# Agent attention and a SoLU feed-forward: the SBUF rings moved to multiples of 512 bytes

## The chip, the cores and the metric

The kernel runs on 1 core of a Trainium2 chip. The metric is the device time of one execution in microseconds (us), as the median of several runs; lower is better.

## What is computed

Agent attention over 4 sequences of 12608 tokens with 128 channels and 49 agents, and then a feed-forward layer with a softmax-gated activation (SoLU) and a layer norm over all 50432 rows:

```python
def sm(a, b):
    s = scale * (a @ b.transpose(0, 2, 1))
    e = np.exp(s - s.max(-1, keepdims=True))
    return e / (e.sum(-1, keepdims=True) + 1e-09)
agent_v = sm(agents, k) @ v
x = (sm(q, agents) @ agent_v).reshape(B * S, D)

h = x @ w_in                                   # 128 -> 1024
e = np.exp(h - np.max(h, axis=-1, keepdims=True))
solu = h * e / (np.sum(e, axis=-1, keepdims=True) + 1e-09)
mu = np.mean(solu, axis=-1, keepdims=True)
var = np.mean((solu - mu) ** 2, axis=-1, keepdims=True)
return ((solu - mu) / np.sqrt(var + 1e-06) * g_ln) @ w_out
```

## The kernel before

The rows are cut into 394 tiles of 128 tokens. For each sequence a first phase (`phase_a`) goes over k and v in chunks of 1024 tokens, held in the rings `kt` and `vt` (for the first sequence in the rings `x` and `t`, which are free then), and leaves agent_v, multiplied into w_in, as a pair of fp16 matrices `mh` and `ml`. A second phase (`phase_b`) makes the softmax of 8 tiles of q (ring `qt`) over the agents and turns it with PE into the fp16 tiles `pT`.

Then each tile runs through one chain. PE multiplies `pT` with `mh` and `ml` into the PSUM tile `ph` (line 953). DVE takes the row minimum and writes the scaled h to `e` (line 981). ACT takes the exponential (line 988). DVE multiplies to `u` (line 996). ACT squares for the variance into `sq` (line 1017). The last product needs u with its features on the partitions. For 343 of the 394 tiles this is done by DMA: POOL (now and then ACT) splits u into a high and a low fp16 half in a tile of the ring `f` (lines 1002 to 1007), and SP issues a DMA transpose from `f` to a tile of the ring `x` (line 1011), 512 KB of fp16 each. PE multiplies `x` with the weights `wh` and `wl` (line 1045). The other tiles are turned by PE into the ring `t` (lines 1024, 1029). DVE scales four tiles into `ob` (line 1092), and SP stores them (line 1096).

All DMAs are issued from SP's one queue, in order. The order of the work on every engine is a stored table (`STEPS`) that `Plan.run` reads; the planner's costs and due times don't set it.

What the change touches is where the tiles lie. Buffers that live throughout are taken one after another from the pool `const`, by `ring` for those that are used in turn. Within a partition each tile starts at the next multiple of 32 bytes behind the one before, so a tile of 4 bytes (one column) takes 32. The large tiles of the rings have 1024, 2048 or 4096 bytes per partition. In the kernel before the first ring, `e`, starts at byte 31200 of a partition, and the eight single columns `su` stand between `u` and `f`:

| tiles | bytes each | first byte before | above a multiple of 512 | of 256 | of 64 |
|---|---|---|---|---|---|
| win_sb, w32 | 4096 | 18816 | 384 | 128 | 0 |
| e, u | 4096 | 31200 | 480 | 224 | 32 |
| f, x, t, kt, vt, qt | 4096 | 64224 | 224 | 224 | 32 |
| ek, eT, ob | 2048 | 174816 | 224 | 224 | 32 |
| pT | 1024 | 183008 | 224 | 224 | 32 |
| mh, ml | 2048 | 202304 | 64 | 64 | 0 |
| sq | 2048 | 212672 | 192 | 192 | 0 |

`mh`, `ml` and `sq` come from other pools, which lie behind `const`. The tiles `ident`, `ones`, `ag_sb`, `wh16` and `wl16` lie ahead of the rings, like `win_sb`, at multiples of 64.

Of the kernel before, what the change touches and what calls it, by code (L numbers as in the profile page):

```python
# [13 lines left out]
F32 = mybir.dt.float32  # L14
# [221 lines left out]
def kernel(  # L236
# [14 lines left out]
    DF = w_in.shape[1]  # L251
    P = 128
    NF = DF // P
    HW = 512
    GT = 4
# [13 lines left out]
    UBUF = 6  # L269
# [4 lines left out]
    UB = 8  # L274
# [73 lines left out]
    const = ctx.enter_context(tc.tile_pool(name="const", bufs=1))  # L348
# [69 lines left out]
    def ring(m, shape, dt, name):  # L418
        return [const.tile(shape, dt, name=f"{name}_{chr(97 + i)}") for i in range(m)]

    er, ur, sur = ring(2, [P, DF], F32, "e"), ring(UBUF, [P, DF], F32, "u"), ring(8, [P, 1], F32, "su")
    fr_, xr, tr = ring(FBUF, [P, 2, DF], F16, "f"), ring(XB, [P, 2 * NF, P], F16, "x"), ring(TBUF, [P, NF, P], F32, "t")
    ktr, vtr, qtr = ring(2, [P, CT * P], F32, "kt"), ring(2, [P, CT * P], F32, "vt"), ring(2, [C, UB * P], F32, "qt")
    ekr, etr, ptr = ring(2, [P, HW], F32, "ek"), ring(2, [P, HW], F32, "eT"), ring(PTB, [P, GT * P], F16, "pT")
    obr, fcr = ring(2, [P, GT, P], F32, "ob"), ring(12, [P, 1], F32, "fc")
    mxr, smr = ring(4, [P, UB], F32, "mx"), ring(4, [P, UB], F32, "sm")
    words = {}
    wi, wo = w_in.bitcast(I32), w_out.bitcast(I32)

# [128 lines left out]
    def both(x):  # L558
        return seq[x][0] % 2 == 1 and seq[x][1] == 0

    mdone, mlast, last_h, ex, CB, cbs = {}, {}, {}, {}, {}, {}
    bmats = {}

# [728 lines left out]
```

## Time and profile before

| | |
|---|---|
| median of 3 runs | 1373.23 us (1370.92 to 1373.4) |
| the profiled execution | 1374.36 us |
| its span, first to last instruction | 1372.6 us |
| PE, DVE, ACT, POOL busy | 90%, 87%, 87%, 84% of the span |
| DMA | 287.70 MB, mean 210 GB/s |
| DMA packets under 512 bytes | 718400 of 753388 |
| granted TensorE clock, mean | 0.977 of full speed |

In the rows below, PE is TensorE's matmuls, PEld its weight loads, DVE VectorE, ACT ScalarE, POOL GpSimd and SP SyncE, which here only issues DMAs. The rows of a line or tile give the count, the shortest, median and longest duration in ns, and when the first and the last one started. The rows of stretches give, after each engine's busy us and count, the granted clock, the share of the 16 DMA engines' time that packets took (above 1 where packets of one engine overlap), and the GB/s moved. "DMA to landing" is the time from the start of the issue to the end of the transfer.

### The profile page before, as it was taken

How to read it: one execution, taken by the hardware profiler on the slowest of the kernel's cores; microseconds unless marked ns; L12 is line 12 of the kernel's file. 1: busy time of each engine (PE TensorE's matmuls, PEld its weight loads, DVE VectorE, ACT ScalarE, POOL GpSimd, SP SyncE). 2: the span in 40 equal slices, each digit the busy share in tenths (PEclk: the TensorE clock that was granted, in tenths of full speed). 3: DMA queues.
4: the chain of work that ended last, by engine and by line, in shares of the span. 5: the costliest groups of instructions: out<-in, count | busy, mean ns of one | idle time of the engine just before them, and what ended most of it. 6: DMA issues, size and time to landing. Idle time of an engine off the chain costs nothing.

```text
span 1372.6 us, 36571 instructions
## 1 busy us (share of the span) xinstructions
PE 1230.9 (90%) x14322; PEld 934.9 (68%) x14322; DVE 1198.8 (87%) x2187; ACT 1198.3 (87%) x2212; POOL 1154.1 (84%) x944
## 2 busy tenths in 40 slices
PE   8889989888988998988998988889989898888987
PEld 4566766666766676766776767666877676676766
DVE  6799979877988898987998897989989899989986
ACT  5699989887989898988989897989989899989997
POOL 3589978887897897887988887988889899989985
PEclk9999999999999999999999999999999999999999
DMA  9599999999999999999989999999999999999997
GB/s 366 183 216 211 240 225 201 235 171 204 194 186 226 223 221 233 216 210 223 185 162 221 216 243 208 213 235 225 212 208 194 192 200 188 206 189 170 194 186 155
DMA packets 753388, 287.70 MB, mean 210 GB/s; under 512 B 718400, under 2 KB 721984, under 8 KB 753216
## 3 DMA queue, kind: packets, MB, share of 16 engines
q1 hardware_dynamic: 753216, 285.38, 104.1%
q8 instruction: 112, 1.84, 0.5%
q14 instruction: 60, 0.49, 0.1%
HBM read 79.67 MB, written 25.82 MB: 77 GB/s over the span
## 4 chain that ended last, share of the span: by engine, by line
DMA 22%; ACT 18%; PE 17%; DVE 15%; POOL 15%; issue 12%; SPq 1%; POOLq 0%; DVEq 0%; ACTq 0%
ACT ph L988 8%; PE px L1045 7%; ACT sq L1017 7%; PE ph L953 5%; DVE e_b L981 4%; POOL f_a L1007 2%; DMA out_dram<-ob_a 2%; DVE e_a L981 2%; DMA x_g<-f_c 2%; POOL f_c L1007 2%; POOL f_d L1007 2%; POOL f_e L1007 2%; DMA x_c<-f_e 2%; PE px L652 2%; DVE u_c L996 1%
## 5 line engine op out<-in xcount | busy, mean ns | idle before, releaser
L981 DVE TENSOR_SCALAR_CACHE_REDUCE e_a<-ph,nk 128x1024 f32<-128x1024 f32 x197 | 251.8, 1278 | 43.7 <-PE ph L953 42.1
L981 DVE TENSOR_SCALAR_CACHE_REDUCE e_b<-ph,nk 128x1024 f32<-128x1024 f32 x197 | 251.8, 1278 | 34.5 <-PE ph L953 32.4
L988 ACT ACTIVATE ph<-e_a,nm 128x1024 f32<-128x1024 f32 x197 | 218.9, 1111 | 42.3 <-DVE e_a L981 41.5
L988 ACT ACTIVATE ph<-e_b,nm 128x1024 f32<-128x1024 f32 x197 | 219.0, 1112 | 38.8 <-DVE e_b L981 37.9
L1045 PE MATMUL px<-wh,x_c 128*128 128x128 f16 x688 | 76.1, 224 | 23.4 <-DMA x_c<-f_e 7.5
L1045 PEld LDWEIGHTS <-x_c 128*128 128x128 f16 x1032 | 64.7, 100 | 39.8 <-DMA x_c<-f_e 8.5
L1045 PE MATMUL px<-wh,x_g 128*128 128x128 f16 x688 | 75.3, 225 | 13.5 <-DMA x_g<-f_c 7.0
L996 DVE SCALAR_TENSOR_TENSOR u_a<-e_a,cb,ph 128x1024 f32<-128x1024 f32 x66 | 84.2, 1275 | 2.7 <-ACT ph L988 1.9
L996 DVE SCALAR_TENSOR_TENSOR u_c<-e_a,cb,ph 128x1024 f32<-128x1024 f32 x65 | 82.8, 1274 | 4.1 <-POOL f_e L1007 1.6
L996 DVE SCALAR_TENSOR_TENSOR u_d<-e_b,cb,ph 128x1024 f32<-128x1024 f32 x66 | 84.1, 1274 | 1.8 <-ACT ph L988 0.8
L996 DVE SCALAR_TENSOR_TENSOR u_f<-e_b,cb,ph 128x1024 f32<-128x1024 f32 x65 | 82.9, 1276 | 2.0 <-ACT ph L988 1.3
L996 DVE SCALAR_TENSOR_TENSOR u_b<-e_b,cb,ph 128x1024 f32<-128x1024 f32 x65 | 82.9, 1275 | 1.4 <-ACT ph L988 1.2
L996 DVE SCALAR_TENSOR_TENSOR u_e<-e_a,cb,ph 128x1024 f32<-128x1024 f32 x65 | 82.9, 1276 | 0.9 <-ACT ph L988 0.3
L1045 PE MATMUL px<-wh,x_e 128*128 128x128 f16 x688 | 74.2, 222 | 10.6 <-DMA x_e<-f_e 3.5
L1045 PEld LDWEIGHTS <-x_g 128*128 128x128 f16 x1032 | 65.3, 101 | 26.2 <-DMA x_g<-f_c 8.1
L1045 PE MATMUL px<-wh,x_f 128*128 128x128 f16 x688 | 72.7, 222 | 9.7 <-DMA x_f<-f_d 4.7
L1045 PEld LDWEIGHTS <-x_e 128*128 128x128 f16 x1032 | 63.4, 99 | 23.3 <-DMA x_e<-f_a 4.4
L1045 PE MATMUL px<-wh,x_a 128*128 128x128 f16 x688 | 73.6, 221 | 6.2 <-DMA x_a<-f_e 3.2
L1045 PE MATMUL px<-wh,x_h 128*128 128x128 f16 x672 | 72.4, 221 | 6.3 <-DMA x_h<-f_d 2.2
L1045 PEld LDWEIGHTS <-x_a 128*128 128x128 f16 x1032 | 63.4, 99 | 21.4 <-issue 6.0
L1045 PE MATMUL px<-wh,x_b 128*128 128x128 f16 x688 | 72.6, 221 | 5.8 <-DMA x_b<-f_b 2.6
L1045 PEld LDWEIGHTS <-x_b 128*128 128x128 f16 x1032 | 63.3, 98 | 20.9 <-issue 5.6
(459 smaller groups left out, 4736.4 us busy)
## 6 DMA issues: line engine op xcount, KB each, us to landing
out_dram<-ob_a SPq DMA_DIRECT2D x49, 256.0 KB, 3.3
out_dram<-ob_b SPq DMA_DIRECT2D x49, 256.0 KB, 3.3
qt_a<-in_qT_dram SPq DMA_DIRECT2D x24, 512.0 KB, 4.8
qt_b<-in_qT_dram SPq DMA_DIRECT2D x24, 512.0 KB, 4.6
kt_b<-in_kT_dram SPq DMA_DIRECT2D x18, 512.0 KB, 4.8
kt_a<-in_kT_dram SPq DMA_DIRECT2D x18, 512.0 KB, 4.6
vt_b<-in_v_dram SPq DMA_DIRECT2D x18, 512.0 KB, 4.7
vt_a<-in_v_dram SPq DMA_DIRECT2D x18, 512.0 KB, 4.9
```

The source lines that it names most:

```text
L652: nc.tensor.matmul(px[h * AP2 : (h + 1) * AP2, :C], eT[:w, o + h * AP2 : o + (h + 1) * AP2], vt[:w, t, :], start=all(z[0] != h for z in mm ...
L953: nc.tensor.matmul(ph[:, sl], w, m[:, sl], start=(q == 0), stop=(q == len(mm) - 1))
L981: nc.vector.tensor_scalar(out=nhs[x], in0=phs[x], scalar1=nks[k][:, j : j + 1], scalar2=None, op0=ALU.mult, op1=ALU.min, accum_out=nms[x])
L988: nc.scalar.activation(out=phs[x], in_=nhs[x], func=AF.Exp, scale=-1.0, bias=nms[x], accum_out=rs_[R]["S"][:, j : j + 1])
L996: nc.vector.scalar_tensor_tensor(out=u, in0=nhs[x], scalar=scal(x)[:, 4:5], in1=phs[x], op0=ALU.mult, op1=ALU.mult, accum_out=su)
L1007: nc.gpsimd.tensor_tensor(out=fs[x][:, 1, :], in0=us[x][0], in1=fs[x][:, 0, :], op=ALU.subtract)
L1017: nc.scalar.activation(out=sq, in_=u, func=AF.Square, bias=su, scale=-float(DF), accum_out=rs_[R]["Q"][:, j : j + 1])
L1045: nc.tensor.matmul(po, ut, wt[:, kf, :], start=(q == 0), stop=(q == len(mm) - 1))
```

## The change

A tile `pad` of 32 bytes per partition is taken from `const` ahead of the rings, and the rings of short tiles (`su`, `fc`, `mx`, `sm`) are taken after all others. Nothing reads or writes `pad`.

```diff
-    er, ur, sur = ring(2, [P, DF], F32, "e"), ring(UBUF, [P, DF], F32, "u"), ring(8, [P, 1], F32, "su")
+    pad = const.tile([P, 8], F32, name="pad")
+    er, ur = ring(2, [P, DF], F32, "e"), ring(UBUF, [P, DF], F32, "u")
     fr_, xr, tr = ring(FBUF, [P, 2, DF], F16, "f"), ring(XB, [P, 2 * NF, P], F16, "x"), ring(TBUF, [P, NF, P], F32, "t")
     ktr, vtr, qtr = ring(2, [P, CT * P], F32, "kt"), ring(2, [P, CT * P], F32, "vt"), ring(2, [C, UB * P], F32, "qt")
     ekr, etr, ptr = ring(2, [P, HW], F32, "ek"), ring(2, [P, HW], F32, "eT"), ring(PTB, [P, GT * P], F16, "pT")
-    obr, fcr = ring(2, [P, GT, P], F32, "ob"), ring(12, [P, 1], F32, "fc")
-    mxr, smr = ring(4, [P, UB], F32, "mx"), ring(4, [P, UB], F32, "sm")
+    obr = ring(2, [P, GT, P], F32, "ob")
...
+    sur, fcr = ring(8, [P, 1], F32, "su"), ring(12, [P, 1], F32, "fc")
+    mxr, smr = ring(4, [P, UB], F32, "mx"), ring(4, [P, UB], F32, "sm")
```

The rings `e`, `u`, `f`, `x`, `t`, `kt`, `vt`, `qt`, `ek`, `eT`, `pT` and `ob` now all start at multiples of 512 bytes: `e` at 31232, `f` at 64000, `ob` at 187904. Behind them `mh` starts at 202336 (96 above a multiple of 256, 32 above one of 64) and `sq` at 212704 (224 above a multiple of 256, 32 above one of 64). What lies ahead of the rings stays. Every engine's list of instructions, SP's DMAs among them, is the same in the same order.

## Rows read from the trace of the kernel before

**Rows 1.** The page: busy us, share of span, instructions of each engine

```profile
PE 1230.9 (90%) x14322; PEld 934.9 (68%) x14322; DVE 1198.8 (87%) x2187; ACT 1198.3 (87%) x2212; POOL 1154.1 (84%) x944
```

**Rows 2.** The page: the chain that ended last, by engine, by line

```profile
DMA 22%; ACT 18%; PE 17%; DVE 15%; POOL 15%; issue 12%; SPq 1%; POOLq 0%; DVEq 0%; ACTq 0%
ACT ph L988 8%; PE px L1045 7%; ACT sq L1017 7%; PE ph L953 5%; DVE e_b L981 4%; POOL f_a L1007 2%; DMA out_dram<-ob_a 2%; DVE e_a L981 2%; DMA x_g<-f_c 2%; POOL f_c L1007 2%; POOL f_d L1007 2%; POOL f_e L1007 2%; DMA x_c<-f_e 2%; PE px L652 2%; DVE u_c L996 1%
```

**Rows 3.** Busy time by stretch: the steady part

```profile
core 0: us, PE busy (x) PEld busy (x) DVE busy (x) ACT busy (x) POOL busy (x), PEclk, DMA share, GB/s
64.00:1300.00 1236.00, 1113.27 (x13110) 851.46 (x13109) 1097.96 (x1981) 1104.20 (x2027) 1072.47 (x855) 0.98 1.07 208
```

**Rows 4.** Line 1011, the transposes: their waiters, issue to landing

```profile
  PEld L1045: 97.4, 69
  PE px L1045: 78.0, 61
...
DMA to landing us min/median/max: 4.2/5.2/9.6
```

**Rows 5.** Tile ob_a: its first waiter, landing of its stores

```profile
  DVE ob_a L1092: 29.3, 13
...
DMA to landing us min/median/max: 1.5/3.2/7.1
```

**Rows 6.** Stretches of the head, 512 KB loads alone

```profile
8.00:12.00 4.00, 4.00 (x22) 2.36 (x21) 2.54 (x9) 2.43 (x5) 0.49 (x1) 1.00 1.02 413
12.00:16.00 4.00, 4.00 (x52) 2.44 (x50) 3.93 (x10) 1.98 (x4) 0.78 (x1) 1.00 1.03 416
24.00:28.00 4.00, 4.00 (x44) 2.50 (x42) 3.48 (x9) 3.52 (x9) 0.64 (x1) 1.00 1.03 410
```

**Rows 7.** Stretches with one late-started transpose alone

```profile
75.95:77.70 1.75, 1.75 (x20) 1.26 (x19) 1.75 (x5) 1.69 (x4) 1.75 (x1) 1.00 1.27 287
367.98:369.82 1.84, 1.22 (x19) 1.12 (x20) 1.75 (x3) 1.84 (x2) 1.61 (x2) 1.00 1.24 280
418.60:420.30 1.70, 1.18 (x19) 1.12 (x20) 1.70 (x5) 1.70 (x4) 1.50 (x5) 1.00 1.27 289
983.85:985.60 1.75, 1.75 (x23) 1.72 (x22) 1.70 (x4) 1.75 (x5) 1.03 (x2) 1.00 1.27 290
```

**Rows 8.** Stretches with one promptly started transpose alone

```profile
79.00:81.40 2.40, 2.33 (x21) 1.06 (x18) 2.40 (x6) 1.96 (x5) 2.40 (x2) 1.00 1.14 212
114.10:116.50 2.40, 2.40 (x35) 1.95 (x33) 2.35 (x5) 2.40 (x5) 2.32 (x3) 1.00 1.13 204
192.10:194.40 2.30, 2.30 (x21) 1.91 (x19) 2.04 (x4) 2.27 (x5) 0.00 (x0) 1.00 1.13 205
224.80:227.20 2.40, 2.40 (x31) 1.76 (x28) 2.40 (x6) 2.37 (x5) 2.40 (x3) 1.00 1.14 210
```

**Rows 9.** SP's DMA issues in time: start, SP time

```profile
77.77 1.88 SPq L1011 DMA_TRANSPOSE x_d<-f_d  x1
...
415.71 3.13 SPq L1011 DMA_TRANSPOSE x_a<-f_d  x1
```

**Rows 10.** Lines 476, 1120: DVE's two 128x1024 maxima, ns min/median/max

```profile
L476 DVE TENSOR_REDUCE wt<-f_e x1: 1209/1209/1209, 52.7 to 52.7; 128x1 f32<-128x1024 f32 x1
...
L1120 DVE TENSOR_REDUCE wm<-win_sb x1: 1211/1211/1211, 27.2 to 27.2; 128x1 f32<-128x1024 f32 x1
```

**Rows 11.** Line 399: POOL's writes of win_sb and f_e, ns

```profile
L399 POOL TENSOR_TENSOR win_sb<-u_b,e_a x2: 1273/1277/1281, 17.9 to 21.7; 128x512 f32<-128x512 f32 x2
...
L399 POOL TENSOR_TENSOR f_e<-u_f,e_a x2: 1268/1271/1274, 37.0 to 38.3; 128x512 f32<-128x512 f32 x2
```

**Rows 12.** ACT by line and form: busy us, mean ns

```profile
L625 ACT ACTIVATE ek_a<-px,nmp 128x512 f32<-128x512 f32 x24 | 16.2, 676 | 4.1 <-DVE nmp L611 2.8 <-PE px L599 1.4
...
L748 ACT ACTIVATE mh<-px,cb 128x512 f16<-128x512 f32 x8 | 5.4, 674 | 1.9 <-PE px L742 1.9
```

**Rows 13.** Lines 742, 599: fp32 matmuls of 512 columns, ns

```profile
L742 PE MATMUL px<-win_sb,av_dup x16: 592/593/677, 49.4 to 1048.4; 128*128 128x512 f32 x16
...
L599 PE MATMUL px<-kt_b,ag_sb x80: 222/593/644, 79.2 to 986.1; 128*64 128x512 f32 x72, 128*64 128x256 f32 x4, 128*64 128x64 f32 x4
```

**Rows 14.** Lines 632, 652: fp32 matmuls of 128 columns, ns

```profile
L632 PE MATMUL px<-ident,ek_a x100: 272/273/330, 11.4 to 984.5; 128*128 128x128 f32 x100
...
L652 PE MATMUL px<-vt_b,eT_b x300: 269/273/325, 104.5 to 1014.1; 128*64 128x128 f32 x148, 64*64 64x128 f32 x2
```

**Rows 15.** Line 953: fp16 matmuls that stream mh and ml, ns

```profile
L953 PE MATMUL ph<-mh,pT_b x160: 376/379/634, 66.1 to 1319.0; 128*128 128x512 f16 x160
L953 PE MATMUL ph<-ml,pT_b x160: 376/379/634, 66.3 to 1319.2; 128*128 128x512 f16 x160
```

## The prediction

> **What bounds the kernel now.** I read the page's busy shares first. PE, DVE, ACT and POOL stand at 90, 87, 87 and 84% of the span [rows 1], so no engine is free enough to give much and none is full. Next the chain that ended last: DMA has 22% of it, ACT 18, PE 17, DVE and POOL 15 each, issue 12 [rows 2]. The chain hops between engines and transfers; it never stays on one. Over the steady part, 64 to 1300 us, DVE is busy 1097.96 of 1236 us, which is 89%, PE 90%, and the DMA share is 1.07 at only 208 GB/s [rows 3]. A share over 1 means that packets of one DMA engine overlap, so the queue is hardly ever empty although few bytes move.
>
> Who waits for DMA? The transposes of line 1011: PE's weight loads wait 97.4 us and its matmuls 78.0 us in total for them, mostly the same time seen twice, and a transpose takes 4.2 us at least and 5.2 in the median from issue to landing [rows 4]. Behind them stand the output stores: DVE waits 29.3 us, 13 times, for a buffer ob_a to be stored [rows 5]. So faster DMA would have somewhere to go, and that is the only place where this change can win anything.
>
> **The change part by part.** The lists of instructions of all five engines are the same row for row; only addresses differ. What lay at 224 above a multiple of 256 (f, x, t, kt, vt, qt, ek, eT, pT, ob; e and u too, at 480 above a multiple of 512) lies at 0. What is allocated behind the large rings moves as well: mh and ml go from 64 to 96 above a multiple of 256, so from a multiple of 64 to 32 beside one; sq does the same. So there are three things to price: engines on realigned tiles, engines on the tiles that lose their multiple of 64, and DMA.
>
> *Engines on realigned tiles.* The trace holds pairs in which one side is already at a multiple of 64 (win_sb, ident, w32, mh) and the other is 32 beside one (f, ek, kt, vt). DVE takes its maximum over 128x1024 of f_e in 1209 ns and of win_sb in 1211 [rows 10]. POOL's product into f_e takes 1271 ns, into win_sb 1277 [rows 11]. ACT writes 512 values into ek_a in 676 ns (mean) and into mh in 674 [rows 12]. PE streams 512 fp32 columns of win_sb in 593 ns and of kt_b in 593 [rows 13], and 128 columns of ident or of vt_b in 273 [rows 14]. The odd side is nowhere slower by more than 2 ns. I take 0 for the realigned tiles; e and u, which no pair holds, are the same kind of operand.
>
> *Engines on mh, ml and sq.* For sq, an ACT write, the pair of rows 12 says 0. For mh and ml no row shows fp16 columns streamed from 32 beside a multiple of 64. The nearest rows are the fp32 pairs, which say 0. I take 0 and keep a price for the third rival below; a gain I exclude, since no pair shows the odd side faster by more than 6 ns in 1271.
>
> *Loads.* While 512 KB loads run alone into the odd addresses, they move 410 to 416 GB/s [rows 6], 1.27 us for one. There is no row of a load into an aligned ring. The best stretch against the middle one is worth under 1%, 0.01 us per load; I take 0, and as an upper end a tenth of a load, 0.13 us, an estimate. The 1.5 us of the quickest store [rows 5] is mostly not wire time: 256 KB at 413 GB/s would be 0.63 us.
>
> *Transposes.* Here the odd address could cost most, since a transpose reads f and writes x, both at 224 above a multiple of 256. Its 512 KB have two speeds with the very same layout. One that starts soon after its issue (x_d<-f_d, issued at 77.77 [rows 9], moving in the stretch from 79.0) runs at 204 to 212 GB/s [rows 8], some 2.5 us. One that had to stand behind another (x_a<-f_d, issued at 415.71 [rows 9], moving from 418.6) runs at 280 to 290 GB/s [rows 7], 1.81 us. So the usual speed isn't the limit of the addresses: something ahead of the data, by inference the supply of descriptors, holds a prompt transpose, and it has the same work after the change. Only late transposes run against the engines' own limit, and only there can alignment show. Lower end: 0. Upper end: the wire speed of the loads, 413 instead of 289 GB/s, which is 1.27 us instead of 1.81, 0.54 us saved per late transpose. I take 0, because the trace shows no sign that the address is what separates 289 from 413; short packets with a fixed cost each would look just the same.
>
> The Trainium skill has a rule that says otherwise: "DMA: Bandwidth & Descriptors", section "How a descriptor splits into AXI transactions", states that a transaction starts at a multiple of 256 bytes, and that a descriptor that starts elsewhere fetches from the boundary below and pays for the unused bytes. For a 256-byte piece at 224 that would be 480 bytes paid for 256, so 413 GB/s would become 220. The trace agrees in half: prompt transposes are below that, but the late ones, at 280 to 290, are well above what it allows.
>
> *The sum.* The profiled execution took 1374.36 us, its span 1372.6, the median of three runs is 1373.23. Engines 0, loads 0, transposes 0: the time stays, 1373 us against the median.
>
> **The rivals.**
>
> *Faster: late transposes speed up.* What speaks for it: DMA is 22% of the chain, 302 us, and less the stores' 2% (27 us) there are 275 us in transfers of about 5.2 us, some 50 links. If every link were late and saved 0.54 us, 27 us would leave the chain. What speaks against it: the floor of 4.2 us isn't touched; DVE is busy 89% of the steady part and PE 90%, so the next wait is close behind. If half of the links are late and half of what they save is passed on, 7 us are left: 1366 us, with 1346 as its extreme. By the rule of the Trainium skill's page "DMA: Bandwidth & Descriptors" quoted above, the full 0.54 us would be had at each late link.
>
> *Slower: mh and ml off their multiple of 64.* Line 953 has 5% of the chain, 69 us, at 379 ns per matmul [rows 15]; DVE's wait for its ph is where it would be seen. If a stream of 512 fp16 columns that starts at an odd 32 bytes cost 5%, 19 ns, 3.4 us would be added: 1377 us. From 4% (15 ns, 394 instead of 379) it decides against "within 0.2%"; at 10%, it is 1380. Against it: both fp32 pairs are equal to the nanosecond.
>
> *It doesn't do what it says.* Each tile starts at the next multiple of 32 bytes, so 32 bytes of pad turn 480 into 0, and all the rings ahead of the moved ones are multiples of 512 long. I give this no chance of its own; its time would be that of no change.
>
> **How the numbers follow.** No change: 0.55. Faster by the transposes: 0.30. Slower by mh and ml: 0.15. A measurement of this kernel can tell about 0.2%, 2.7 us, from no change. The runs before span 1370.92 to 1373.4, so a no-change case lies in 1370 to 1376. From the rival cases and a little scatter of the first: faster by over 0.2% 0.32, within 0.2% 0.52, slower 0.16. For 8 in 10 the range runs from 1359, inside the faster rival, past the slower rival's 1377. The likeliest case gives 1373.
>
> **What would show it.** If I am right, rows like [rows 7] and [rows 8] stay at about 285 and 208 GB/s, the landing of line 1011 at 4.2 and 5.2 us, the DMA share of the steady part at 1.07, and line 953 at 379 ns. If the first rival holds, the late transposes rise above 300 GB/s and the DMA share falls clearly below 1.07 while the bytes stay; PE's wait on line 1045 then shrinks, and so does DVE's for ob_a. If prompt transposes speed up too, my reading that they are held ahead of the data is wrong, and the gain could pass the rival's 7 us. If the second rival holds, line 953 rises above 394 ns with DMA as it was.

## The result, and the profile after

The time fell from 1372.1 to 1338.35 us (medians of 4 runs each). One run of the change, the profiled one (1351.65 us), was in a slower state of the chip, so the ratio is that of the other runs: 0.974, with an interval of 0.970 to 0.978. Six runs of the same kernel on another occasion gave 1337.23 us (median) against 1372.74, a ratio of 0.975 (0.972 to 0.978). This lies below the range on record, which began at 1359, and below the first rival's extreme of 1346. The rows below are those of the profiled execution of that repetition (1339.88 us, span 1338.1). All line numbers are 2 higher than before.

The page of the changed kernel: busy us by engine, and the chain that ended last, by engine and by line.

```profile
PE 1220.5 (91%) x14322; PEld 928.5 (69%) x14322; DVE 1198.5 (90%) x2187; ACT 1198.1 (90%) x2212; POOL 1154.8 (86%) x944
...
ACT 21%; DMA 20%; POOL 18%; DVE 14%; PE 13%; issue 13%; SPq 1%; POOLq 0%; DVEq 0%; ACTq 0%
ACT ph L990 9%; ACT sq L1019 8%; PE px L1047 5%; PE ph L955 4%; DVE e_b L983 3%; POOL f_a L1009 2%; POOL f_c L1009 2%; DVE e_a L983 2%; POOL f_d L1009 2%; DMA x_g<-f_c 2%; POOL f_e L1009 2%; POOL f_b L1009 1%; DVE u_a L998 1%; PE px L654 1%; DMA x_c<-f_a 1%
```

Busy us have hardly moved from [rows 1] (DVE 1198.8 to 1198.5, POOL 1154.1 to 1154.8; PE 1230.9 to 1220.5, at a mean granted clock of 0.985 instead of 0.977). The clock isn't the cause: at 0.985 the runs of the change took 1334 to 1340 us, and two runs at 0.985 of a kernel without the gain (the one with f and x put back, below) 1367 and 1370. So the work is nearly as long as it was. What went is waiting: DVE's idle time, span less busy, was 1372.6 - 1198.8 = 173.8 us and is 1338.1 - 1198.5 = 139.6. That is 34 us, the whole gain. DMA has 20% of the chain instead of 22% [rows 2].

The transposes (line 1013 now): who waited for them (us, times), and issue to landing.

```profile
  PEld L1047: 80.0, 57
  PE px L1047: 64.0, 50
...
DMA to landing us min/median/max: 3.6/4.8/10.6
```

Tile ob_a: its first waiter (us, times), and the landing of its stores.

```profile
  DVE ob_a L1094: 21.8, 11
...
DMA to landing us min/median/max: 1.5/3.0/6.4
```

The quickest transpose lands after 3.6 us instead of 4.2, the median after 4.8 instead of 5.2, and PE's matmuls wait 64.0 us for them instead of 78.0 [rows 4]. DVE's wait for ob_a fell from 29.3 to 21.8 us [rows 5].

Stretches with one late-started transpose alone (busy us by engine, granted clock, DMA share, GB/s):

```profile
76.25:78.00 1.75, 1.75 (x19) 1.26 (x18) 1.75 (x5) 1.72 (x4) 1.75 (x1) 1.00 1.28 290
395.40:397.10 1.70, 1.08 (x16) 1.09 (x17) 1.03 (x2) 1.67 (x4) 1.70 (x2) 0.88 1.28 291
673.95:675.70 1.75, 1.69 (x23) 1.03 (x24) 0.81 (x3) 1.72 (x3) 1.75 (x3) 1.00 1.27 288
```

Stretches with one promptly started transpose alone, in the same columns:

```profile
79.40:81.30 1.90, 1.83 (x15) 0.74 (x13) 1.90 (x5) 1.46 (x5) 1.90 (x1) 1.00 1.21 277
114.30:116.20 1.90, 1.90 (x33) 1.67 (x30) 1.90 (x3) 1.90 (x4) 1.82 (x2) 1.00 1.19 270
665.50:667.30 1.80, 1.80 (x31) 1.79 (x28) 1.80 (x4) 1.80 (x3) 1.80 (x1) 1.00 1.23 280
```

The late ones run at 288 to 291 GB/s, as [rows 7] did at 280 to 290. The prompt ones run at 270 to 280, where [rows 8] stood at 204 to 212. This is the change in one view: the prompt transposes, which stood at some 208 GB/s, now come near the speed of these late ones, which is as before. "Late" needs a distinction, though. All late stretches shown come from queues with loads or stores in them. Sorted by what was still in flight when they were issued (in the trace of before; the order is the same in both), the 129 transposes with a load ahead of them land as late as before, to 0.01 us in the mean. The 145 with nothing but other transposes ahead land 0.70 us sooner (4.35 instead of 5.05), the 10 with nothing ahead 0.60 sooner, and the 59 with a store but no load ahead 0.37. So most transposes that gain were queued, and behind other transposes.

The steady part in one window (its first line names the columns):

```profile
core 0: us, PE busy (x) PEld busy (x) DVE busy (x) ACT busy (x) POOL busy (x), PEclk, DMA share, GB/s
64.00:1266.00 1202.00, 1101.74 (x13065) 843.44 (x13066) 1093.80 (x1974) 1100.07 (x2019) 1069.10 (x852) 0.99 1.05 214
```

Stretches of the head with loads alone, in the same columns:

```profile
8.00:12.00 4.00, 4.00 (x19) 1.88 (x18) 2.04 (x8) 2.54 (x5) 0.83 (x1) 0.63 1.03 422
12.00:16.00 4.00, 4.00 (x52) 2.40 (x49) 3.93 (x12) 1.98 (x4) 0.44 (x1) 1.00 1.04 424
```

Line 955 (once 953), instructions of one form with min, median and max in ns:

```profile
L955 PE MATMUL ph<-mh,pT_b x160: 376/379/634, 65.9 to 1288.1; 128*128 128x512 f16 x160
L955 PE MATMUL ph<-ml,pT_b x160: 377/379/634, 66.2 to 1288.4; 128*128 128x512 f16 x160
```

The loads of the head went from 410 to 416 GB/s [rows 6] to 422 to 424, about 2%, which is 0.03 us for 512 KB (1.24 instead of 1.27). That this comes from the addresses isn't shown: the same stretches have 412 to 421 GB/s in the run below that leaves the loads' rings x and t at 224. The matmuls that stream mh and ml from 32 beside a multiple of 64 still take 379 ns in the median [rows 15]. The DMA share of the steady part went from 1.07 to 1.05 while the bytes per us rose from 208 to 214 [rows 3].

### The profile page after: what moved, and what is told of

The parts are those of the page before. It is cut to its first block, busy times and chain, and to the rows that moved or that the text cites. A ratio compares the mean times of both kernels' runs of the same rounds, so it can differ in the third digit from the quotient of the medians.

```text
span 1349.8 us, 36571 instructions
## 1 busy us (share of the span) xinstructions
PE 1229.9 (91%) x14322; PEld 934.5 (69%) x14322; DVE 1199.6 (89%) x2187; ACT 1196.4 (89%) x2212; POOL 1155.2 (86%) x944
## 2 busy tenths in 40 slices
DMA packets 753388, 287.70 MB, mean 213 GB/s; under 512 B 718400, under 2 KB 721984, under 8 KB 753216
## 4 chain that ended last, share of the span: by engine, by line
DMA 21%; ACT 19%; POOL 18%; PE 17%; DVE 13%; issue 11%; SPq 1%; POOLq 0%; DVEq 0%; ACTq 0%
ACT ph L990 8%; ACT sq L1019 7%; PE px L1047 7%; PE ph L955 5%; DVE e_b L983 3%; POOL f_d L1009 2%; POOL f_a L1009 2%; POOL f_c L1009 2%; POOL f_e L1009 2%; DVE e_a L983 2%; PE px L654 2%; DMA out_dram<-ob_a 2%; POOL f_b L1009 2%; PE px L601 1%; DMA x_g<-f_e 1%
## 5 line engine op out<-in xcount | busy, mean ns | idle before, releaser
L1047 PE MATMUL px<-wh,x_d 128*128 128x128 f16 x688 | 72.9, 220 | 7.2 <-DMA x_d<-f_b 4.4
L1047 PEld LDWEIGHTS <-x_d 128*128 128x128 f16 x1032 | 63.7, 98 | 20.1 <-DMA x_d<-f_b 4.7
```

The lines of the kernel that those rows point to most:

```text
L1047: nc.tensor.matmul(po, ut, wt[:, kf, :], start=(q == 0), stop=(q == len(mm) - 1))
```

## The experiments

Four of the runs below are small kernels that do transfers alone, each executed once, and their landings come from that one execution.

Theory A: a transpose that starts promptly depends on where its tiles lie, and that alone is the gain. Theory B: the gain comes from loads, stores or engines.

**Transposes alone.** A kernel without attention and feed-forward, which issues only transposes of 512 KB, five one at a time and then seven queued closely for each pair of offsets:

```python
def t_32_0(k): nc.sync.dma_start_transpose(out=dv(k, 0), in_=sv(32))
def t_0_32(k): nc.sync.dma_start_transpose(out=dv(k, 32), in_=sv(0))
...
def several(f):
    for r in range(5):
        f(0)
    for k in (1, 2, 3, 1, 2, 3, 0):
        f(k)
```

> No attention and no feed-forward here: only DMA transposes of 512 KB within SBUF, one line of code for each pair of byte offsets of source and destination (0, 32, 64, 128, 224, 256 above a multiple of 512), 5 one at a time and then 6 queued closely. Theory A (a prompt transpose depends on where its tiles lie): 224/224 lands 4.2 us after issue at least, as line 1011 did before the change, and 0/0 3.6 us, as after it; one of source and destination alone, or both, carries the 0.6 us. Theory B (the gain in the kernel came from elsewhere: loads, stores, engines): all pairs land within 0.1 us of each other. If the multiple of 256 is what counts, 64 and 128 are as slow as 224, and 256 as fast as 0; if 64 is what counts, only 32 and 224 are slow.

Three of its source lines: the time that the issue held its queue (min, median, max in ns) and the landing: source at 0 and at 224 with the destination at 0 (lines 44 and 48), and source at 0 with the destination at 224 (line 53). The first queued transpose writes `dst_b`, the last one `dst_a`. The landings are those of all twelve; the table has every pair.

```profile
L44 SPq DMA_TRANSPOSE dst_a<-src x6: 1317/1594/1953, 3.3 to 32.3; - x6
L44 SPq DMA_TRANSPOSE dst_b<-src x2: 1737/2179/2621, 19.4 to 25.9; - x2
...
DMA to landing us min/median/max: 3.6/4.0/4.4
...
L48 SPq DMA_TRANSPOSE dst_a<-src x6: 1317/1850/2627, 153.2 to 187.5; - x6
L48 SPq DMA_TRANSPOSE dst_b<-src x2: 2090/2846/3602, 171.6 to 179.8; - x2
...
DMA to landing us min/median/max: 4.2/4.6/5.6
...
L53 SPq DMA_TRANSPOSE dst_a<-src x6: 1317/1591/2153, 322.6 to 351.8; - x6
...
DMA to landing us min/median/max: 3.6/3.9/4.3
```

| source, destination above a multiple of 512 | us to landing, min / median / max |
|---|---|
| 0, 0 | 3.6 / 4.0 / 4.4 |
| 256, 0 | 3.6 / 4.0 / 4.6 |
| 32, 0 | 4.3 / 4.5 / 5.6 |
| 64, 0 | 4.2 / 4.6 / 5.5 |
| 128, 0 | 4.2 / 4.5 / 5.6 |
| 224, 0 | 4.2 / 4.6 / 5.6 |
| 0, 32 and 0, 64 and 0, 224 | 3.6 / 3.9 / 4.3 |
| 0, 128 and 0, 256 | 3.6 / 4.0 / 4.4 and 3.6 / 4.0 / 4.3 |
| 32, 32 and 224, 224 | 4.3 / 4.5 / 5.6 and 4.2 / 4.5 / 5.6 |
| 64, 64 and 128, 128 | 4.2 / 4.5 / 5.6 and 4.2 / 4.4 / 5.6 |
| 256, 256 | 3.6 / 3.9 / 4.5 |

Theory A, and more sharply than put: only the source counts, a multiple of 256 is enough, and each of the four offsets tried in between costs the same 0.6 us (in the median, single ones land after 3.7 us from 0 and 4.3 from 224). These are the very 3.6 and 4.2 us of the kernel's transposes after and before. A part of it shows on the queue already: issues from 224 hold it for 1850 ns in the median, those from 0 for 1594. The queued seven pay as well. They start 2.1 us apart from 0 (19.4 to 32.3 in six steps) and 2.6 apart from 224 (171.6 to 187.5), and land after 4.0 to 4.4 and 4.6 to 5.6 us. So a transpose behind other transposes isn't free of the address: each costs the queue 0.5 us more. The page "DMA: Bandwidth & Descriptors" of the Trainium skill (section "How a descriptor splits into AXI transactions") has the boundary right: pieces that start off a multiple of 256 bytes pay. It has them pay for the unused bytes, so by an estimate from its rule a 256-byte piece at 32 should cost much less than one at 224; by these rows they cost the same.

**The change with f and x put back at 224.** In the kernel, everything else stays at multiples of 512:

```diff
-    fr_, xr, tr = ring(FBUF, [P, 2, DF], F16, "f"), ring(XB, [P, 2 * NF, P], F16, "x"), ring(TBUF, [P, NF, P], F32, "t")
+    const.tile([P, 56], F32, name="pad_f")
+    fr_ = ring(FBUF, [P, 2, DF], F16, "f")
+    xr = ring(XB, [P, 2 * NF, P], F16, "x")
+    const.tile([P, 72], F32, name="pad_t")
+    tr = ring(TBUF, [P, NF, P], F32, "t")
```

> The changed kernel once more, for a closer interval and as the measure for the other runs on the same chip. All theories: about 1336 us, 0.974 of before; prompt transposes land at 3.6 us at least.

The repetition gave 1337.23 us, 0.975 of before, and 3.6 us for the quickest transpose; its rows are those of the result.

> The change with the rings f and x alone put back at 224 above a multiple of 512; all others stay at multiples of 512. Theory A (the transposes carry all): the gain is gone, 0.998 to 1.002 of before, line of the transposes lands at 4.2 us at least. Theory B (loads, stores or engines): 0.974 as with the whole change.

PE's wait for the transposes, and their landing, with f and x off:

```profile
  PE px L1051: 76.1, 57
...
DMA to landing us min/median/max: 4.3/5.2/9.4
```

0.999 of before (0.997 to 1.002): the gain is gone, and with it the 3.6 us.

**Only f and x at multiples of 512.** The pads are placed the other way round; e, u, t and all that follow stand as before the change:

```diff
-    pad = const.tile([P, 8], F32, name="pad")
...
+    const.tile([P, 8], F32, name="pad_f")
+    fr_ = ring(FBUF, [P, 2, DF], F16, "f")
+    xr = ring(XB, [P, 2 * NF, P], F16, "x")
+    const.tile([P, 56], F32, name="pad_t")
```

> Only f and x at multiples of 512; e, u, t, kt, vt, qt, ek, eT, pT, ob where they were before the change (480 or 224 above one). Theory A (the transposes carry all): 0.974 of before. Theory B: 1.0. If both have a part, in between, and this run and the one with f and x off add up to the whole.

PE's wait for the transposes and their landing:

```profile
  PE px L1050: 61.1, 48
...
DMA to landing us min/median/max: 3.6/4.6/11.2
```

0.975 (0.971 to 0.979), as the whole change. The two runs add up, and theory B is out: loads, stores and engines have no part that can be seen.

**Only f, at 256.** The rings e and u at 480, f at 256, x and the rest at 224 above a multiple of 512:

```diff
-    pad = const.tile([P, 8], F32, name="pad")
...
+    const.tile([P, 72], F32, name="pad_f")
+    fr_ = ring(FBUF, [P, 2, DF], F16, "f")
+    const.tile([P, 120], F32, name="pad_x")
+    xr = ring(XB, [P, 2 * NF, P], F16, "x")
```

> Only the ring f is moved, to 256 above a multiple of 512; all other rings stand where they stood before the change (x, t and the rest at 224, e and u at 480). Theory A1 (the read of the transpose's source must start at a multiple of 256, nothing else counts): 0.975 of before, as the whole change. Theory A2 (512 is needed, or x too): 1.0.

The same two lines of the trace here:

```profile
  PE px L1050: 62.9, 48
...
DMA to landing us min/median/max: 3.6/4.7/9.4
```

0.976 (0.973 to 0.979). Of twelve kinds of rings that were moved, five tiles of f are what counts, and 512 was not needed.

**The change with f alone put back at 224.**

```diff
+    const.tile([P, 56], F32, name="pad_f")
+    fr_ = ring(FBUF, [P, 2, DF], F16, "f")
+    const.tile([P, 72], F32, name="pad_x")
+    xr = ring(XB, [P, 2 * NF, P], F16, "x")
```

> The change with the ring f alone put back at 224; x and all others at multiples of 512. Theory A1: 0.998 to 1.002 of before, transposes land at 4.2 us at least. Theory A2 (x has a part): between 0.975 and 1.0.

The same two lines with f off alone:

```profile
  PE px L1051: 81.7, 64
...
DMA to landing us min/median/max: 4.3/5.2/9.7
```

1.000 (0.998 to 1.002): x at a multiple of 512 brings nothing.

**Two of the five tiles of f at 224.**

```diff
+    fr_ = ring(3, [P, 2, DF], F16, "f")
+    const.tile([P, 56], F32, name="pad_f")
+    fr_ += [const.tile([P, 2, DF], F16, name=f"f_{z}") for z in "de"]
+    const.tile([P, 72], F32, name="pad_x")
```

> The change with two of the five tiles of f (d, e) at 224, three at a multiple of 512. If each transpose adds its own part to the path: three fifths of the gain, 0.985 of before, 1352 us. If the slow ones set the pace of the queue: 0.995 to 1.0. If the first saving is the one that matters and the rest is slack: 0.975 to 0.980.

The same two lines with f_d and f_e off:

```profile
  PE px L1051: 71.3, 52
...
DMA to landing us min/median/max: 3.6/4.9/10.3
```

0.982 (0.979 to 0.984), 1348.57 us. Three of five tiles bring 1.8 of 2.5%, somewhat more than three fifths (0.985, just outside the interval), and far from the case in which the two odd tiles set the pace (0.995 to 1.0). The transposes add their parts, roughly in proportion to their number.

**Late transposes, loads and stores.** A kernel without attention and feed-forward; transposes behind two loads, and single copies:

```python
def first(k): nc.sync.dma_start(out=dst[k].bitcast(F32)[:, :1024], in_=kT[0, :, :1024])
def second(): nc.sync.dma_start(out=ld[:, :1024], in_=kT[0, :, 1024:2048])
def late_0(k): nc.sync.dma_start_transpose(out=dv(k), in_=src[:, :2048])
def late_224(k): nc.sync.dma_start_transpose(out=dv(k), in_=src[:, 112:2160])
```

> No attention and no feed-forward here. Transposes issued behind two 512 KB loads, from a source at 0 and at 224 above a multiple of 512, by turns; then single loads into SBUF at 0 and at 224, and single 256 KB stores from 0 and from 224. Theory S (the odd source slows what goes ahead of the data, the drain itself is the same): late transposes from 0 and from 224 land within 0.15 us of each other, both moving near 290 GB/s. Theory R (the engines read an odd source more slowly): the late ones differ by 0.6 us, as the prompt ones did. Loads differ by less than 0.1 us either way. Stores read 2048 bytes at a time: by theory R they gain a ninth of 0.6 us or less, by S nothing.

The late transposes, from 0 (line 45) and from 224 (line 46):

```profile
L45 SPq DMA_TRANSPOSE dst_b<-src x6: 4348/4718/5026, 5.7 to 125.1; - x6
...
DMA to landing us min/median/max: 6.3/6.7/7.0
...
L46 SPq DMA_TRANSPOSE dst_b<-src x6: 4162/4368/4582, 51.3 to 169.2; - x6
...
DMA to landing us min/median/max: 6.1/6.4/6.6
```

The late transpose from 224 isn't slower; it lands 0.3 us earlier (6.4 against 6.7). So theory R, that the engines read an odd source more slowly, falls: once the pieces flow they flow alike, at 286 GB/s for the first transpose from 0 and 287 for the first from 224 (from 10.0 to 11.0 and from 55.6 to 56.6 us). Theory S holds but for that 0.3, which is more than the 0.15 it allowed. The trace shows where the 0.3 lies: the load just ahead lands after 5.3 us in the median when a transpose from 0 follows it and after 4.9 when one from 224 does, and from then on both need the same 1.9 us. By inference, the pieces from 0 are ready sooner and move among those of the load. Loads and stores of long pieces don't care: loads into 0 land after 3.4, 3.6 and 3.8 us (min, median, max) and into 224 after 3.4, 3.5 and 3.6; stores from 0 after 2.0 and from 224 after 2.0 in the median.

**Behind five loads.** The kernel before this with three more loads ahead of each transpose:

```diff
             second()
+            for i in range(3):
+                nc.sync.dma_start(out=more[i], in_=kT[i + 1, :, :1024])
             f((r + 1) % 2)
```

> No attention and no feed-forward here. Transposes from a source at 0 and at 224, by turns, issued behind five 512 KB loads instead of two, so that all that goes ahead of the data has some 6 us of time. If the odd source costs nothing once that is done: both land within 0.1 us of each other, moving at 280 to 290 GB/s. If the engines read an odd source more slowly: 0.6 us apart. If the even source is really behind when queued, as the run with two loads hinted (0.3 us), it is behind here too.

The landing of the transposes, from 0 (line 46) and from 224 (line 47):

```profile
L46 SPq DMA_TRANSPOSE dst_b<-src x6: 6852/7105/7242, 6.9 to 188.7; - x6
...
DMA to landing us min/median/max: 8.8/9.0/9.3
...
L47 SPq DMA_TRANSPOSE dst_b<-src x6: 6532/6666/6922, 75.4 to 257.1; - x6
...
DMA to landing us min/median/max: 8.4/8.7/9.1
```

9.0 us from 0 and 8.7 from 224: again nothing is lost by the odd source, and again the even one is 0.3 us behind, not within the 0.1 expected. Here too both need the same 1.9 us from the landing of the load ahead. Behind loads, the odd address is free.

**Sizes, and plain copies of the same pieces.** A kernel without attention and feed-forward, each of its transfers eight times alone:

```python
def pieces(t, o):
    return t[:, o // 2 : o // 2 + 4096].rearrange("p (a t) -> p a t", t=256)[:, :, :P]
def turn_512_224(): nc.sync.dma_start_transpose(out=tv(512), in_=src[:, 112:624])
...
def copy_224_0(): nc.sync.dma_start(out=pieces(dst, 0), in_=pieces(src, 224))
```

> No attention and no feed-forward here. One at a time: transposes of 512, 1024 and 2048 fp16 columns (128, 256, 512 KB) from a source at 0 and at 224; then plain copies within SBUF of the same 2048 pieces of 256 bytes, source and destination at 0 or 224. If each source piece that crosses a multiple of 256 costs its own part, the difference grows with size: 0.15, 0.3, 0.6 us. If it is a fixed cost per transfer: 0.6 us at each size. If plain copies of 256-byte pieces obey the same rule of the source, copy 224 to 0 and 224 to 224 land some 0.6 us later than 0 to 0 and 0 to 224; if the price belongs to transposes, all four copies land together.

The plain copies of 2048 pieces of 256 bytes, from source to destination: 0 to 0 (line 49), 224 to 0 (50) and 0 to 224 (51).

```profile
L49 SPq DMA_DIRECT2D dst<-src x8: 593/594/704, 154.0 to 179.0; - x8
...
DMA to landing us min/median/max: 3.5/3.5/3.7
...
L50 SPq DMA_DIRECT2D dst<-src x8: 593/594/594, 182.5 to 211.3; - x8
...
DMA to landing us min/median/max: 4.1/4.1/4.1
...
L51 SPq DMA_DIRECT2D dst<-src x8: 593/594/594, 215.3 to 244.2; - x8
...
DMA to landing us min/median/max: 4.1/4.1/4.1
```

Transposes of 512, 1024 and 2048 columns land after 2.3, 2.7 and 3.6 us (medians) from 0, and after 2.4, 3.1 and 4.3 from 224. So the price is 0.1, 0.4 and 0.7 us for 128, 256 and 512 KB: it grows with the number of pieces, some 0.3 ns for each of the 2048. (No other short length was tried.) The packet records of this run tell where it lies: the first piece of a 512 KB transpose starts 1.2 us after the issue from either source, and the last one ends after 3.2 us from 0 and 3.8 from 224. A transpose from an odd source doesn't start later; its pieces come more slowly. Plain copies pay the same 0.6 us for an odd source, and, unlike transposes, for an odd destination too, but only once for both (224 to 224: 4.1). Whether for the same reason, no run tells.

## Why the prediction was wrong

*What it had right.* The engines cost nothing on either side: line 955 has its 379 ns, the rival of mh and ml fell, and no engine's busy time rose by more than 0.7 us. Loads measured 2% faster, inside the tenth allowed for, and by the run with f and x put back nothing of it reaches the time. The place, the transposes and behind them the stores of ob, was named as the only one that could win. The reading of [rows 7] against [rows 8] is borne out in half. The runs behind two and five loads show the drain, the moving of pieces that are ready, to be free of the address. That a prompt transpose is held by something other than the drain fits them; but it isn't over before the data starts, since the first piece leaves after 1.2 us from either source.

*The step that failed* is the next sentence of that part: that what holds a prompt transpose "has the same work after the change". Two speeds with the same layout show that the address isn't the limit of the drain. They say nothing on whether the thing that holds a prompt one depends on the address. It does, by 0.6 us for each prompt transpose of 2048 pieces and by 0.5 for each in a queue of transposes; the term was taken as 0. There was no row in the trace of before of a transpose from a multiple of 256, so both ends should have stayed open for the prompt ones too.

*The first rival had the right part and the wrong half.* It gave its gain to the late transposes (0.54 us each, at half of the links) and left the floor of 4.2 us alone. The floor fell to 3.6; of those that queue, the ones behind other transposes gained 0.70 us in the mean, and only those behind a load gained nothing. Its links were counted wrongly too: the chain of before holds 37 transposes of 6.4 us in the mean (237.5 us), not 50 of 5.2. So 50 links at 0.6 us, 30 us, would have come close to the 34 or 35 measured by luck. How the savings add up to 34 us isn't shown: the chain of the change holds 34 transposes with 222.7 us, only 15 less, and the run with two odd tiles shows just that the parts add up roughly in proportion. The last part of the prediction did name this outcome, prompt transposes that speed up, and said that the gain could then pass 7 us.

*The rule of the Trainium skill* ("DMA: Bandwidth & Descriptors", section "How a descriptor splits into AXI transactions") was quoted and set aside, since the late stretches broke the limit of 220 GB/s worked out from it. Its boundary was right for the transposes that pay; what it charges, bytes fetched in vain, isn't what the runs show. "The trace agrees in half" should have been the reason to give the other half a chance of more than 0.30.

What it is that holds back the pieces of a prompt transpose (the making of their descriptors is a guess), and why a piece that crosses a multiple of 256 takes longer there, no run shows: the count of packets under 512 bytes is 718400 before and after.

## What to carry to other kernels

A DMA that moves many pieces of 256 bytes within SBUF (no other short length was tried) should have its source at a multiple of 256 bytes, and a plain copy its destination too; the check is the position of the tile within the partition, and single-column tiles between large rings are what spoils it. Two speeds of one kind of transfer in a trace tell that two limits exist; before one of them is called independent of a change, it has to be seen with the change, for which a small kernel that does the transfer alone is enough. And "late" is no single case: behind a load the odd address cost nothing here, behind another transpose 0.5 us. Ask what stands ahead in the queue before a saving is given to the late ones or to the prompt ones.

## What the runs showed of the hardware that was not expected

- Transposes of 512 KB within SBUF: 3.6 us at least from issue to landing with the source at a multiple of 256 bytes, 4.2 or 4.3 with it at 32, 64, 128 or 224; the destination doesn't count.
- In a queue of such transposes, one starts every 2.1 us from a source at 0 and every 2.6 from one at 224.
- Plain copies of 256-byte pieces pay for either side, 3.5 against 4.1 us, and not twice.
- Behind two or five loads the odd source costs nothing: 1.9 us from the landing of the load ahead, as from an even one. The load ahead of an odd one landed 0.4 us sooner (4.9 against 5.3 us, behind two loads), and the odd transpose so 0.3 us earlier.
- Loads of 512 KB into 0 and 224 (3.6 and 3.5 us) and stores of 256 KB (2.0 and 2.0) are alike.
